# Windowed attention and a SiLU feed-forward layer on one core: new loads for batch 0, and pieces of batches 1 and 2 moved among blocks of 256

## The chip, the cores and the metric

The kernel runs on one core of a Trainium2 chip. The core has five engines that run their own queues of instructions in order and wait for each other by semaphores: TensorE (PE, matrix products and transposes), VectorE (DVE), ScalarE (ACT), GpSimd (POOL, which here mostly issues loads) and SyncE (SP, which issues stores). Transfers run on 16 DMA engines. The metric is the device time of one execution in microseconds; less is better. Before the change the median of 3 runs is 331.06 us (330.93 to 331.69).

## What is computed

Attention over 8 batches, 8 heads, 576 tokens and 64 elements a head. In heads 0 to 3 a token sees itself and the 31 tokens before it ("plain"). In heads 4 to 7 it sees every fourth token of the last 128 ("strided"): tokens of one residue modulo 4 form a class of 144, and within a class the window is again 32. The result, 4608 rows of 512, goes through a feed-forward layer with SiLU.

```python
rel = pos[:, None] - pos[None, :]
mask_plain = (rel >= 0) & (rel < 32)
mask_dil = (rel >= 0) & (rel < 128) & (rel % 4 == 0)
scores = np.where(mask, scale * q @ k.T, -1e9)
attn = np.exp(scores - scores.max(-1))
attn = attn / (attn.sum(-1) + 1e-9)
x = (attn @ v)                        # 4608 x 512
h = x @ w_in                          # 512 -> 2048
out = (h / (1 + np.exp(-h))) @ w_out  # 2048 -> 512
```

## The kernel before

**Attention.** q and k of a batch are loaded by GpSimd's queue (with a cast to float16) into `n` tiles, several tokens a partition (`load_qk`, L102; batch 0 in two parts of 256 and 320 tokens with 8 tokens a partition, `load_qk0`, L114). TensorE transposes them into PSUM (`transpose`, L260; batch 0: `transpose0`, L288 and L296). Copies bring them to `kT`, `qT` (plain) or `kC`, `qC` (strided). For later batches the copies are `both`: half 0 by VectorE, half 1 by ScalarE. A score block is 32 queries by 64 keys, four blocks above each other on the partitions (`score` L306, `score_class` L318). VectorE scales and adds the mask (L369, L379 for batch 0; L415, L424) and takes the negated maximum of each block (L389, L431). Then `exps` has two forms. Without `shift`, ScalarE runs one exp for each block of 64 columns with the maximum as bias and the sum as a second output (L459, each with an instruction that reads the sum). With `shift` (L441), VectorE subtracts the maxima first, ScalarE runs one exp over all blocks (L453), and VectorE sums afterwards (L468). `normal` divides (L472, L473, L475), `turn` transposes the weights (L484), `turned` copies them (L492), `values` multiplies by V (L517; batch 0: L543; the last 64 tokens: L580), `finish` copies the result to `xT` (L593; batch 0: L556).

**V.** `vw` holds V in windows of 64 rows. `load_v` (L123, L131, L136) fills the upper half of the partitions; `shift_v` (L146, L151, L154, L156) copies rows from there to the lower half by SBUF-to-SBUF DMAs, on SP's queue for batches 0 and 1. `clear_v` zeroes the rows that no load fills.

**Feed-forward.** `layer1` multiplies by `w_in` (L606, SiLU on ScalarE L614; batch 0 in two parts, L625 and L632), with two PSUM tiles `h`. `layer2` multiplies by `w_out` (L666, for batch 0 L642), `store` copies out and SP stores (L651, L652). Even batches have 4 row tiles in the second layer, odd ones 5.

**Order.** It is written out by hand. Batch 0's attention up to the first values stands ahead of the loop. After that, attention of later batches is put between the matmuls of the feed-forward layers: `plan_of(b)` fills a list of steps, and `plan(s)` issues what is due. Steps 0 to 15 are the 16 blocks of the first layer of batch b, steps from 16 on are groups of 4 matmuls of its second layer. What is added first at a step is issued first. In steps 15 to 18 of batch 1:

```python
transposes(at, 3, 0, 15)
at(17, load_qk, 4)
at(14, scores, 2, 1)
all_exps(2, 0)      # at step 16
all_exps(2, 1)      # at step 16
at(17, scores, 3, 0)
at(18, exps, 3, 0, 0)
at(18, exps, 3, 0, 1)
```

PSUM holds two `big` tiles (h, o and batch 0's scores) and four `ps` tiles (transposes, scores, values). `keep_busy` issues matmuls whose result nobody reads. A load on GpSimd's queue waits until the eighth load before it has landed.

Of the kernel before, what the change touches and what calls it, by code (L numbers as in the profile page):

```python
# [22 lines left out]
UR = 8  # L23
# [4 lines left out]
def kernel(  # L28
# [62 lines left out]
    def load_qk(b):  # L91

        for which in (0, 1):
            t = nat.tile([P, H * UR, D], F16, tag=f"n{which}", name=f"n{which}_{b}")
# [12 lines left out]
    def load_qk0(part):  # L107

        t0, n = ((0, PA), (SA, PB))[part]
        qk0[part] = [None, None]  # L110
        for which, src in ((1, k), (0, q)):
            t = nat.tile([P, H * UR, D], F16, tag=f"n{which}", name=f"n{which}_0{part}")
            t = qk0[part][which] = t.rearrange("p (h u) d -> p h u d", h=H)
            nc.gpsimd.dma_start(  # L114
                out=t[0:n],
                in_=src[0, :, t0 : t0 + n * UR].rearrange("h (p u) d -> p h (u d)", u=UR),
            )
# [23 lines left out]
    def shift_v(b, queue, parts):  # L141
# [3 lines left out]
        for m0, m1, n in parts:  # L145
            queue.dma_start(  # L146
                out=vw[W:KB, NP + n.start * ND : NP + n.stop * ND],
                in_=vw[KB : KB + W, NP + n.start * ND : NP + n.stop * ND],
            )
            if n.stop == 2:  # L150
# [3 lines left out]
            queue.dma_start(out=f[W:KB, :, m0:m1], in_=f[KB : KB + W, :, m0:m1])  # L154
            l0 = max(m0, 1)
            queue.dma_start(out=f[0:W, :, l0:m1], in_=f[KB + W : P, :, l0 - 1 : m1 - 1])  # L156

    FIRST, REST, ALL = (0, 4, slice(0, 1)), (4, NM, slice(1, 2)), (0, NM, slice(0, 2))
# [36 lines left out]
    load_qk0(0)  # L195
    make_identity(nc, ident)

# [8 lines left out]
    load_qk0(1)  # L206
    load_v(0, ("first", "plain"))
    load_w_in(0)
    load_v(0, ("second", "short"))
    shift_v(0, nc.sync, (FIRST, REST))  # L210
    clear_v(1, nc.gpsimd)
    for c in range(1, 4):
        load_w_in(c)
# [222 lines left out]
    def shift(b, z, hi):  # L436
# [4 lines left out]
        nc.vector.tensor_tensor(  # L441
# [248 lines left out]
    def plan_of(b):  # L690
# [9 lines left out]
        if b == 0:  # L700
# [16 lines left out]
            at(10, scores, 1, 1)  # L717
            for hi in (0, 1):
                at(10, shift, 1, 1, hi)
            transposes(at, 1, 0, 13)  # L720
            at(17, scores, 1, 0)
# [5 lines left out]
            for hi in (0, 1):  # L727
                at(17, exps, 1, 0, hi)
            later(at, 1, 1, (18, 20, 24, 26))
            later(at, 1, 0, (22, 25, 28, 30))  # L730
        elif b == 1:
            at(16, load_v, 3)
            at(16, shift_v, 3, nc.gpsimd, (ALL,))
            transposes(at, 2, 0, 4)
            transposes(at, 2, 1, 10)
            transposes(at, 3, 0, 15)
            at(7, scores, 2, 0)
            at(17, load_qk, 4)
            at(14, scores, 2, 1)
            all_exps(2, 0)  # L740
            all_exps(2, 1)
            at(17, scores, 3, 0)
            at(18, exps, 3, 0, 0)
            at(18, exps, 3, 0, 1)
            later(at, 2, 0, (22, 24, 27, 28))
            later(at, 2, 1, (29, 31, 33, 34))
        else:
# [36 lines left out]
    def keep_busy(n):  # L784

        busy = big.tile([P, 2, 512], F32, tag="big", name="busy")
        four = ident[:, None, :].broadcast_to([P, 4, P])
        for _ in range(n):
            nc.tensor.matmul(busy[:, 0].rearrange("p (n c) -> p n c", n=4), ident, four, start=True, stop=True)

    load_qk(1)
    load_w_out(0)
# [4 lines left out]

    transposes0(0, 1, (act, dve))
    scores0(1, 0)
    transposes0(0, 0, (act, dve))  # L800
    exps(0, 1, 0)
    scores0(0, 0)
    transposes0(1, 1, (act, dve))
    exps(0, 0, 0)
    normal(0, 1, 0)
    scores0(1, 1)
    turn(0, 1, 0)
    turned(0, 1, 0, act)
    transposes0(1, 0, (act, act))
    normal(0, 0, 0)  # L810
    turn(0, 0, 0)
    turned(0, 0, 0, act)
    shift(0, 1, 1)
# [60 lines left out]
```

## Time and profile before

| what | us |
|---|---|
| median of 3 runs (range) | 331.06 (330.93 to 331.69) |
| the profiled execution | 331.63 |
| its span, first to last instruction | 329.8 |
| TensorE busy | 311.1 (94%) |
| ScalarE busy | 214.8 (65%) |
| VectorE busy | 180.2 (55%) |
| GpSimd busy | 86.0 (26%) |
| first matmul of the first layer (L625) starts | 25.69 |
| second layer of batch 0 (L642) starts | 47.68 |
| first layer of batch 1 (L606) starts | 67.36 |
| second layer of batch 1 (L666) starts | 89.06 |

In the rows of the profile a line names engine, source line, operation and tiles ("t<-ident,n": t is written from ident and n), then the count. In the row of slices, 40 equal pieces of 8.2 us, a digit is the busy share in tenths. In a table of stretches each row has from and to, the length, and busy time with the number of instructions for TensorE, its weight loads, VectorE, ScalarE and GpSimd, then the granted TensorE clock, the share of the DMA engines and GB/s. In a timeline, a row has start, length, and in brackets the idle time of the engine before it with what ended it. The source lines named in this section are those of the kernel before.

### The profile page before, as it was taken

The page shows a single profiled execution, that of the slowest core. Times are in us where ns is not written, and L with a number is a line of the kernel's source. Part 1 is how long each engine was busy: PE and PEld are TensorE (multiplying, and loading weights), DVE is VectorE, ACT ScalarE, POOL GpSimd, SP SyncE. Part 2 cuts the span into 40 slices and gives each one's busy share as a digit, 9 for nine tenths or more (in the row PEclk, how much of TensorE's full clock was granted, in tenths as well). Part 3 has the DMA queues.
Part 4 walks back from the last instruction along what each step waited for, and adds up shares of the span by engine and source line. Part 5 has one row for each costly group of instructions (what it writes and reads, how often), then busy time and mean ns, then how long its engine had stood idle before and what let it go on. Part 6 is the DMA issues. An engine that isn't in the chain of part 4 may idle for free.

```text
span 329.8 us, 11976 instructions
## 1 busy us (share of the span) xinstructions
PE 311.1 (94%) x5238; PEld 203.1 (62%) x5238; DVE 180.2 (55%) x377; ACT 214.8 (65%) x714; POOL 86.0 (26%) x144
## 2 busy tenths in 40 slices
PE   1679999999899999999999999999999999999996
PEld 1547764577545777467845677468755676467644
DVE  5778379745578744774557444774557442540011
ACT  2746669156599847985699357995699447916400
POOL 8743645544500560056004430042000000000000
PEclk9999999999999999999999999999999999999999
DMA  6999999999911975199404990175001100110022
GB/s 92 168 216 198 166 204 210 191 204 107 166 47 70 137 108 98 67 107 175 70 34 92 177 143 6 64 101 108 2 34 66 66 4 1 64 66 2 0 76 86
DMA packets 45141, 32.90 MB, mean 100 GB/s; under 512 B 21824, under 2 KB 39744, under 8 KB 45088
## 3 DMA queue, kind: packets, MB, share of 16 engines
q0 software_dynamic: 38752, 21.74, 48.5%
q1 hardware_dynamic: 6336, 10.39, 8.8%
q8 instruction: 41, 0.67, 0.9%
q14 instruction: 12, 0.10, 0.1%
HBM read 37.75 MB, written 9.44 MB: 143 GB/s over the span
## 4 chain that ended last, share of the span: by engine, by line
PE 79%; DMA 10%; DVE 4%; ACT 3%; POOL 2%; issue 2%; POOLq 0%
PE h L606 34%; PE o L666 31%; DMA n<-in_k_dram 4%; DMA vw<-in_v_dram 3%; PE t L260 3%; DMA n<-in_q_dram 3%; PE x L517 3%; PE pt L484 2%; ACT pe L459 2%; PE o L642 2%; PE s L318 1%; PE s L306 1%; DVE ms L415 1%; DVE pn L475 1%; DVE nm L431 1%
## 5 line engine op out<-in xcount | busy, mean ns | idle before, releaser
L614 ACT ACTIVATE gT<-h 128x576 f16<-128x576 f32 x112 | 72.8, 650 | 72.1 <-PE h L606 71.4
L606 PE MATMUL h<-xT,w_in 128*128 128x288 f16 x896 | 115.5, 286 | 0.8 <-issue 0.4
L666 PE MATMUL o<-w_out,gT 128*128 128x512 f16 (+1 forms) x528 | 115.6, 373 | 0.0
L606 PEld LDWEIGHTS <-w_in 128*128 128x128 f16 x896 | 85.7, 98 | 24.0 <-issue 1.3
L459 ACT ACTIVATE pe<-ms,nm 128x64 f32<-128x64 f32 x262 | 86.9, 334 | 0.1
L666 PEld LDWEIGHTS <-gT 128*128 128x128 f16 x528 | 50.0, 98 | 53.0
L651 DVE COPY ob<-o 128x512 f32<-128x512 f32 (+1 forms) x37 | 24.9, 674 | 53.6 <-PE o L666 53.1
L459 ACT ACTIVATION_READ_ACCUMULATOR pe<-ms,nm 128x1 f32 x262 | 49.2, 188 | 0.0
L415 DVE SCALAR_TENSOR_TENSOR ms<-s,mask 128x512 f32<-128x512 f32 x28 | 19.2, 686 | 39.1 <-PE ss L306 19.0
L123 POOL DMA_DIRECT2D vw<-in_v_dram x16 | 10.0, 632 | 84.8 <-PE x L517 84.3
L475 DVE TENSOR_TENSOR pn<-pe,r 128x640 f16<-128x640 f32 (+2 forms) x32 | 25.3, 792 | 1.1
L593 DVE CAST xT<-x 128x512 f16<-128x512 f32 x28 | 18.0, 686 | 11.7 <-PE xs L580 11.7
L431 DVE TENSOR_REDUCE nm<-ms 128x10 f32<-128x640 f32 (+1 forms) x28 | 22.0, 787 | 1.0
L102 POOL DMA_DIRECT2D n<-in_q_dram x28 | 16.4, 605 | 13.5 <-DMA w_in<-in_moe_w_in_dram 5.7
L102 POOL DMA_DIRECT2D n<-in_k_dram x28 | 16.5, 604 | 8.1 <-DMA w_in<-in_moe_w_in_dram 2.8
L492 DVE COPY ptT<-pt 128x640 f16<-128x640 f16 (+2 forms) x30 | 13.1, 472 | 9.9 <-PE pt L484 9.7
L625 PE MATMUL h<-xT,w_in 128*128 128x256 f16 (+1 forms) x128 | 17.8, 293 | 0.0
L632 ACT ACTIVATE gT<-h 128x512 f16<-128x512 f32 (+1 forms) x16 | 10.4, 650 | 8.1 <-PE h L625 7.9
L642 PE MATMUL o<-w_out,gT 128*128 128x512 f16 x64 | 14.8, 379 | 0.0
L625 PEld LDWEIGHTS <-w_in 128*128 128x128 f16 x128 | 12.3, 100 | 3.8 <-issue 0.5
L260 PEld LDWEIGHTS <-n 64*64 64x64 f16 (+1 forms) x840 | 10.0, 101 | 6.4 <-issue 5.1
L484 PE MATMUL pt<-ident,pn 128*128 128x128 f16 x152 | 12.2, 224 | 1.7 <-DVE pn L475 1.7
(84 smaller groups left out, 261.6 us busy)
## 6 DMA issues: line engine op xcount, KB each, us to landing
out_dram<-ob SPq DMA_DIRECT2D x35, 256.0 KB, 2.0
n<-in_k_dram POOLq DMA_DIRECT2D x28, 144.0 KB, 5.4
n<-in_q_dram POOLq DMA_DIRECT2D x28, 144.0 KB, 5.7
vw<-in_v_dram POOLq DMA_DIRECT2D x8, 288.0 KB, 7.0
vw<-in_v_dram POOLq DMA_DIRECT2D x16, 128.0 KB, 4.4
w_in<-in_moe_w_in_dram POOLq DMA_DIRECT2D x4, 512.0 KB, 12.5
w_out<-in_moe_w_out_dram POOLq DMA_DIRECT2D x4, 512.0 KB, 11.3
vw<-vw POOLq DMA_DIRECT2D x12, 128.0 KB, 3.7
```

The lines of the kernel that those rows point to most:

```text
L102: nc.gpsimd.dma_start(out=qk[b, z, which][i * HF : i * HF + UPS[z]].rearrange("p h u d -> p h (u d)"), in_=src[b, h : h + 2].rearrange("h ...
L260: nc.tensor.transpose(dst, w, ident[r, r])
L415: nc.vector.scalar_tensor_tensor(out=ms[:, 0:8].rearrange("p (n t) c -> p n (t c)", n=2), in0=s[hi].rearrange("p n t c -> p n (t c)"), sca ...
L431: nc.vector.tensor_reduce(out=nm[:, 0:w], in_=ms[:, 0:w], axis=AX.X, op=ALU.max, negate=True)
L459: nc.scalar.activation(pe[:, t, :], ms[:, t, :], AF.Exp, bias=nm[:, t : t + 1], accum_out=l[:, t : t + 1],)
L475: nc.vector.tensor_tensor(pn[:, 0:w], a["pe", z, hi][:, 0:w], r[:, 0:w, None].broadcast_to([P, w, KB]), ALU.mult)
L606: nc.tensor.matmul(h[:, half, 0:HS], w_in16[:, c, f * P : f * P + P], xT[:, c, half * HS : half * HS + HS], start=(c == 0), stop=(c == MC ...
L614: nc.scalar.activation(gT[:, f, s0 : s0 + S].rearrange("p (a c) -> p a c", a=2), h[:, :, 0:HS], AF.Silu)
L625: nc.tensor.matmul(h[:, i, 0 : c1 - c0], w_in16[:, c, (f + i) * P : (f + i + 1) * P], xT[:, c, c0:c1], start=(c == 0), stop=(c == MC - 1),)
L642: nc.tensor.matmul(o, gT[:, f, t * P : (t + 1) * P], w_out16[:, f, :], start=(f == 0), stop=(f == NFF - 1),)
L651: nc.vector.tensor_copy(ob, o)
L666: nc.tensor.matmul(o[:, 0, 0:m], gT[:, f, t * P : (t + 1) * P], w_out16[:, f, cols], start=(f == 0), stop=(f == NFF - 1),)
```

## The change

Batch 0's q and k come with 4 tokens a partition instead of 8: 64 and 80 partitions instead of 32 and 40, in pieces of 1 KB instead of 2 KB; in the first part the strided heads are loaded ahead of the plain ones, in DMAs of their own. The first four plain windows of batch 0's V are shifted by two VectorE copies instead of two DMAs. GpSimd subtracts the maxima of (0, plain, part 0), which had none subtracted before, and of (0, strided, part 1). The order of batch 0's attention is new, the first values are plain ones, both exps of part 1 stand after the first `finish`, and `keep_busy` is gone. On GpSimd's queue w_in 1 stands behind its first subtraction, w_in 2 and 3 behind its second; `load_qk(1)` and `clear_v(1)` follow these. In the plan of batch 0, batch 1's plain transposes go from step 13 to 17 and their scores from 17 to 20, with VectorE subtracting the second maximum; in the plan of batch 1, batch 3's plain transposes go from step 15 to 17, their scores from 17 to 20, their exps from 18 to 21. Some other steps move by one.

```diff
-UR = 8
+UR = 4
...
-    def load_qk0(part):
+    def load_qk0(part, kinds):
...
+        for h in kinds:
+            for which, src in ((1, k), (0, q)):
+                nc.gpsimd.dma_start(
+                    out=qk0[part][which][0:n, h].rearrange("p h u d -> p h (u d)"),
+                    in_=src[0, h, t0 : t0 + n * UR].rearrange("h (p u) d -> p h (u d)", u=UR),
+                )
...
+            move = getattr(queue, "dma_start", None) if queue in (nc.sync, nc.gpsimd) else queue.tensor_copy
+            move(out=f[W:KB, :, m0:m1], in_=f[KB : KB + W, :, m0:m1])
             l0 = max(m0, 1)
-            queue.dma_start(out=f[0:W, :, l0:m1], in_=f[KB + W : P, :, l0 - 1 : m1 - 1])
-
-    FIRST, REST, ALL = (0, 4, slice(0, 1)), (4, NM, slice(1, 2)), (0, NM, slice(0, 2))
+            move(out=f[0:W, :, l0:m1], in_=f[KB + W : P, :, l0 - 1 : m1 - 1])
+
+    FIRST, REST, ALL = (0, 4, None), (4, NM, slice(1, 2)), (0, NM, slice(0, 2))
+    STRIDED_FIRST = (0, 0, slice(0, 1))
...
-    load_qk0(0)
+    load_qk0(0, (STRIDED,))
     make_identity(nc, ident)
+    load_qk0(0, (PLAIN,))
...
-    load_qk0(1)
+    load_qk0(1, (slice(0, H),))
     load_v(0, ("first", "plain"))
+    shift_v(0, nc.sync, (STRIDED_FIRST,))
     load_w_in(0)
     load_v(0, ("second", "short"))
-    shift_v(0, nc.sync, (FIRST, REST))
-    clear_v(1, nc.gpsimd)
-    for c in range(1, 4):
-        load_w_in(c)
+    shift_v(0, nc.sync, (REST,))
...
-    def shift(b, z, hi):
+    def shift(b, z, hi, engine=nc.vector):
...
-            at(10, scores, 1, 1)
+            at(8, scores, 1, 1)
             for hi in (0, 1):
-                at(10, shift, 1, 1, hi)
-            transposes(at, 1, 0, 13)
-            at(17, scores, 1, 0)
+                at(8, shift, 1, 1, hi)
+            transposes(at, 1, 0, 17)
+            at(20, scores, 1, 0)
+            at(20, shift, 1, 0, 1)
...
             for hi in (0, 1):
-                at(17, exps, 1, 0, hi)
+                at(20, exps, 1, 0, hi)
             later(at, 1, 1, (18, 20, 24, 26))
-            later(at, 1, 0, (22, 25, 28, 30))
+            later(at, 1, 0, (25, 26, 28, 30))
...
-            transposes(at, 2, 0, 4)
+            transposes(at, 2, 0, 3)
             transposes(at, 2, 1, 10)
-            transposes(at, 3, 0, 15)
-            at(7, scores, 2, 0)
+            transposes(at, 3, 0, 17)
+            at(8, scores, 2, 0)
             at(17, load_qk, 4)
-            at(14, scores, 2, 1)
+            at(13, scores, 2, 1)
             all_exps(2, 0)
             all_exps(2, 1)
-            at(17, scores, 3, 0)
-            at(18, exps, 3, 0, 0)
-            at(18, exps, 3, 0, 1)
+            at(20, scores, 3, 0)
+            at(21, exps, 3, 0, 0)
+            at(21, exps, 3, 0, 1)
...
-                at(9, scores, b + 1, 1)
+                at(10, scores, b + 1, 1)
...
-                transposes(at, b + 2, 1, 30)
+                transposes(at, b + 2, 1, 31)
...
+    transposes0(0, 1, (act, dve))
+    scores0(1, 0)
+    transposes0(0, 0, (act, dve))
+    exps(0, 1, 0)
+    scores0(0, 0)
+    shift(0, 0, 0, nc.gpsimd)
+    load_w_in(1)
+    transposes0(1, 1, (act, act))
+    exps(0, 0, 0)
+    transposes0(1, 0, (act, act))
+    normal(0, 1, 0)
+    normal(0, 0, 0)
+    scores0(1, 1)
+    shift(0, 1, 1, nc.gpsimd)
+    for c in (2, 3):
+        load_w_in(c)
+    turn(0, 1, 0)
+    turned(0, 1, 0, act)
+    shift_v(0, nc.vector, (FIRST,))
+    scores0(0, 1)
+    turn(0, 0, 0)
+    turned(0, 0, 0, act)
+    shift(0, 0, 1)
+    values0(0, 0)
+    finish0(0, 0, (act, act))
+    values0(1, 0)
+    finish0(1, 0, (act, act))
+    exps(0, 1, 1)
+    exps(0, 0, 1)
     load_qk(1)
+    clear_v(1, nc.gpsimd)
     load_w_out(0)
     load_w_out(1)
     load_v(1)
     load_w_out(2)
     load_w_out(3)
...
     load_qk(2)
```

More of the change, by code (lines that the diff above doesn't have):

```diff
@@ L93, in load_qk @@
         for which in (0, 1):
-            t = nat.tile([P, H * UR, D], F16, tag=f"n{which}", name=f"n{which}_{b}")
+            t = nat.tile([P, 2 * sum(URS), D], F16, tag=f"n{which}", name=f"n{which}_{b}")
             u0, u1 = 2 * URS[0], 2 * (URS[0] + URS[1])
@@ L105, in load_qk @@
                     )
-    def load_qk0(part):
+    def load_qk0(part, kinds):
         t0, n = ((0, PA), (SA, PB))[part]
[L110 to L117, printed above, removed]
+        if part not in qk0:
+            tiles = [nat.tile([P, 2 * sum(URS), D], F16, tag=f"n{w}", name=f"n{w}_0{part}") for w in (0, 1)]
+            qk0[part] = [t[:, 0 : H * UR].rearrange("p (h u) d -> p h u d", h=H) for t in tiles]
+        for h in kinds:
[4 more added lines that the diff above has]
+                )
     def load_v(b, pieces=("first", "second", "short", "plain")):
@@ L145, in shift_v @@
         for m0, m1, n in parts:
[L146 to L150, printed above, removed]
+            if n:
+                queue.dma_start(
+                    out=vw[W:KB, NP + n.start * ND : NP + n.stop * ND],
+                    in_=vw[KB : KB + W, NP + n.start * ND : NP + n.stop * ND],
+                )
+            if n and n.stop == 2:
                 queue.dma_start(
@@ L153, in shift_v @@
                 )
-            queue.dma_start(out=f[W:KB, :, m0:m1], in_=f[KB : KB + W, :, m0:m1])
+            if m1 == m0:
+                continue
+            move = getattr(queue, "dma_start", None) if queue in (nc.sync, nc.gpsimd) else queue.tensor_copy
+            move(out=f[W:KB, :, m0:m1], in_=f[KB : KB + W, :, m0:m1])
             l0 = max(m0, 1)
-            queue.dma_start(out=f[0:W, :, l0:m1], in_=f[KB + W : P, :, l0 - 1 : m1 - 1])
-    FIRST, REST, ALL = (0, 4, slice(0, 1)), (4, NM, slice(1, 2)), (0, NM, slice(0, 2))
+            move(out=f[0:W, :, l0:m1], in_=f[KB + W : P, :, l0 - 1 : m1 - 1])
+    FIRST, REST, ALL = (0, 4, None), (4, NM, slice(1, 2)), (0, NM, slice(0, 2))
+    STRIDED_FIRST = (0, 0, slice(0, 1))
     def plain_v(a, j, h):
@@ L194 @@
     clear_v(0, nc.vector)
-    load_qk0(0)
+    PLAIN, STRIDED = slice(0, HH), slice(HH, H)
+    load_qk0(0, (STRIDED,))
     make_identity(nc, ident)
+    load_qk0(0, (PLAIN,))
     nc.gpsimd.affine_select(
@@ L440, in shift @@
         ms, nm = a["ms", z, hi], a["nm", z, hi]
-        nc.vector.tensor_tensor(
+        engine.tensor_tensor(
             ms[:, 0:w], ms[:, 0:w], nm[:, 0:w, None].broadcast_to([P, w, KB]), ALU.add
@@ L782, in transposes0 @@
                 transpose0(part, 2 * z + i, which, copies[which])
[L784 to L789, printed above, removed]
+    transposes0(0, 1, (act, dve))
[27 more added lines that the diff above has]
+    exps(0, 0, 1)
     load_qk(1)
+    clear_v(1, nc.gpsimd)
     load_w_out(0)
@@ L796 @@
     load_w_out(3)
[L798 to L813, printed above, removed]
-    exps(0, 1, 1)
-    scores0(0, 1)
-    shift(0, 0, 1)
-    keep_busy(4)
-    values0(1, 0)
-    finish0(1, 0, (dve, act))
-    values0(0, 0)
-    finish0(0, 0, (dve, act))
-    exps(0, 0, 1)
-    keep_busy(2)
     load_qk(2)
```

## The prediction, made before the changed kernel ran

> **What bounds the kernel now.** First the busy times and the slices of the page, then the stretches, to see where TensorE stands still.
>
> ```profile
> PE 311.1 (94%) x5238; PEld 203.1 (62%) x5238; DVE 180.2 (55%) x377; ACT 214.8 (65%) x714; POOL 86.0 (26%) x144
> ...
> PE   1679999999899999999999999999999999999996
> ...
> DMA  6999999999911975199404990175001100110022
> ```
>
> ```profile
> 0.00:10.00 10.00, 3.29 (x120) 2.95 (x122) 5.65 (x24) 1.93 (x3) 8.75 (x20) 1.00 0.78 105
> 10.00:20.00 10.00, 6.87 (x239) 5.38 (x236) 7.78 (x17) 8.83 (x42) 5.87 (x8) 1.00 1.46 184
> 20.00:25.69 5.69, 3.96 (x86) 1.65 (x76) 3.75 (x7) 2.11 (x5) 2.29 (x4) 1.00 1.22 219
> ...
> 66.70:89.00 22.30, 20.59 (x474) 15.67 (x473) 11.60 (x20) 13.06 (x21) 12.30 (x21) 1.00 1.04 156
> 89.00:110.00 21.00, 21.00 (x327) 10.80 (x326) 14.76 (x34) 20.69 (x115) 1.89 (x4) 1.00 0.27 73
> ```
>
> TensorE is the bound from 25.69 us, where the first layer starts, and its idle time (18.7 us of 329.8) lies mostly before that. What can be won is that start, and 1.7 us between 66.7 and 89. The last line is the one to keep: from 89 to 110, the second layer of batch 1, TensorE has no idle time at all and ScalarE works 20.69 of 21.00 us. The timeline there, TensorE and then ScalarE:
>
> ```profile
> 85.47 0.48 PE L260 MATMUL t<-ident,n 64*64 64x64 f16 x36
> 86.86 0.67 PE L260 MATMUL t<-ident,n 64*64 64x64 f16 x36 [0.91 <-DVE ms L415]
> 87.46 0.91 PE L606 MATMUL h<-xT,w_in 128*128 128x288 f16 x6
> 88.82 0.41 PE L606 MATMUL h<-xT,w_in 128*128 128x288 f16 x2 [0.45 <-issue]
> 89.06 1.02 PE L666 MATMUL o<-w_out,gT 128*128 128x512 f16 x4
> 90.02 0.68 PE L306 MATMUL s<-kT,qT 64*32 64x64 f16 x64
> ```
>
> ```profile
> 89.26 0.65 ACT L614 ACTIVATE gT<-h 128x576 f16<-128x576 f32 x1 [0.96 <-PE h L606]
> 89.93 1.28 ACT L459 ACT_TABLE_LOAD   x1
> 91.22 0.35 ACT L459 ACTIVATE pe<-ms,nm 128x64 f32<-128x64 f32 x1
> ```
>
> ```profile
> L459 ACT ACTIVATE pe<-ms,nm 128x64 f32<-128x64 f32 x56 | 18.6, 337 | 0.0
> ```
>
> Batch 3's plain transposes (step 15) wait 0.91 us for buffers that VectorE still reads. Their copies on ScalarE are done before the table load at 89.93; then 56 exps run without a gap, the last starting at 109.46: (109.46 − 91.22) / 55 = 0.332 us each.
>
> **The decisive part: batch 3's transposes go from step 15 to 17.** `exps` of batch 2 stay at step 16: 8 + 10 + 10 + 10 = 38 exps with a bias for each block. `transposes` uses `both`: half 0 is copied by VectorE, half 1 by ScalarE. At step 17 the two ScalarE copies (kT, qT) stand behind the 38 exps on an engine that works in order; the built order of the changed kernel shows table load, x8, x10, x10, x10, kT, qT. TensorE meets `scores(3, 0)` at step 20, and those read half 1. Let L be the start of this second layer (89.06 before). TensorE gets there after 4 matmuls (0.86), 72 transposes (0.76 at 71.44 in the chain) and 12 matmuls (2.60): L + 4.2. ScalarE starts its exps at 91.22 − 89.06 = L + 2.16, needs 38 × 0.332 = 12.6, then two copies (72.02 to 73.20, 1.2): L + 16.0. TensorE stands **11.8 us**. Bounds 11.0 (half 0's scores go first, copies overlap) and 12.5 (the exps' own 337 ns, 12.8, and full copies). Behind the blocked scores stand all later second-layer matmuls; before, none had slack, so nothing takes this back.
>
> After such a pause the matmuls may run at half pace. The start of the trace shows it, though the granted clock reads 1.00:
>
> ```profile
> 22.07 1.89 PE L789 MATMUL busy<-ident 128*128 128x512 f16 x4
> ```
>
> Four matmuls of 512 columns take 1.89 us there and 1.02 at 89.06. The slow pace lasted until about 26.5 (4 first-layer matmuls from 25.69 to 26.50, 5 in the next 0.5), 4.4 us in all, of which 3.5 dense. Bounds 0 and 2.2 (half of 4.4); I take 1.7, half of the dense part, the nearest row. The Trainium skill (TensorE: Matmul & The Clock Gate, Part 1) says that an idle window of about 3.4 us halves the clock until a window as long has been busy. By that rule the pause here costs 1.7, without it 0; the slow start agrees, and no pause of this length in mid-kernel is in this trace.
>
> **The start.** Loads: the first part is 64 rows of 4 tokens instead of 32 of 8, strided heads first, so transposes halve (16 for 0.61 before, 8 now; plain 64 for 1.89, 32 now). GpSimd issues two more DMAs (2 × 0.66 by its rows) ahead of the band, which stays in front of the first mask-add. k,q of part 1 keep their bytes at twice the descriptors; on each of the 16 engines v's first 16 pieces of 1 KB took 1.0 (it landed at 14.4, q01 at 13.4), 62 ns a piece, and w_in's 32 pieces of 2 KB 3.4 (landings near 23.7, 27.0, 30.6), 106 ns: 2304 pieces at 62 instead of 1152 at 106 are +1.3. Against that, 80 rows divide evenly among 16 engines and 40 do not (k01 was used 4.1 after q00, q01 only 2.3 after k01). I put q01 at 12.8 instead of 13.4; bounds 11.5 and 14.7.
>
> Chain from there, durations of equal instructions before: part-1 copies on ScalarE to 14.0 (two of 0.4 after the transposes); exp(0,0) 0.65 to 14.7; VectorE sum, add, reciprocal, product 0.69 + 0.17 + 0.20 + 0.69, with gaps to 16.5; (1,1) mask-add and maximum 0.6 + 0.45 + 0.95 to 18.5; the two V copies that replace DMAs; (0,1) mask-add 0.6 + 0.3, which frees the buffer that the second values need; values 0.65, two copies on ScalarE 0.8. V copies of 1024 and 768 elements: by the 512-element copy L222 (0.43) 0.86 + 0.65; the lower bound is two of the 64-element copies L221 (0.213 each), 0.4, the upper 0.96 + 0.72 (memset L190, 0.485 for 512). The SP queue loses the two plain shifts (issued at 16.86 and 17.56), and the strided one, alone now, lands its median 5.3 after v's 13.8, before the values. The six filler matmuls (2.9 us) lay in the wait for those shifts: 0. I take 1.5 for the copies: first layer at 22.5, **−3.2** (bounds −5.0 and +0.5).
>
> GpSimd's subtractions of 512 and 768 columns: lower bound VectorE's own 0.69 and 0.95, upper twice its select's rate (0.287 for 128), 2.3 and 3.4; I take that rate once, 1.2 and 1.7. The Trainium skill (GPSIMD Engine Reference, Performance versus the Vector engine) gives 2.6 cycles an element for two inputs, by which 1.1 and 1.7 would be my estimate; no run here shows it. The first is hidden under the eight exps of (1,0) (2.7 us) and the wait for q01; the second under the V copies and (0,1). But w_in 2 and 3 are queued behind the second: issue at about 20.4 and 21.2 instead of 13.70 and 14.76. Cover: the DMA queue is full until w_in 1 lands (23.7, the wait that ends at 23.72 on GpSimd), so they still land near 27 and 30.6; needed at about 28.6 and 31.5. The clear of vw1 (3.3) now stands before w_out 0; batch 1's q,k keep the queue full meanwhile: 0.
>
> **First layer, batch 0.** ScalarE now runs exps (1,1) and (0,1), 0.85 + 0.74, and the table load 1.28 before its first silu: 2.9 after the layer's start, against 27.38 − 25.69 = 1.7. With two h buffers TensorE follows: **+1.2**. Batch 1's plain transposes leave step 13, where they waited 0.80 at 45.02: **−0.8**; their own 0.95 is paid at step 17: 0. Batch 3's load waits on GpSimd for them, but its turn came at 54.38 anyway: 0.
>
> **Second layer, batch 0.** `scores(1, 0)` at step 20 wait for ScalarE (silu, table 1.28, two exps 1.4, copies 1.2): about 0.35. VectorE then has mask-adds, maxima and the new subtraction (3.9 us) ahead of `normal(1,1,1)` (2.05), so `turn` at 24 waits about 2.0 (0.77 before); `normal(1,0,1)`, now at 26 behind the copies of `values`, makes `turn` at 28 wait about 1.7. New 4.05 less old 0.44 + 0.77 + 0.39: **+2.4** (bounds 0 and 4).
>
> **First layer, batch 1.** Without transposes at 15 the waits 0.91 and 0.45 go: **−1.36**. Scores and transposes moved by one step (batch 2 on, and 9 to 10, 30 to 31 later) stand beside a TensorE without waits: 0, bounds ±0.5.
>
> **Sum.** −3.2 + 1.2 − 0.8 + 2.4 − 1.36 + 11.8 + 1.7 = +11.7. The profiled execution took 331.63 (span 329.8 and 1.83 around it), so 343.4; the median of the runs shown is 0.57 lower: **342.8**.
>
> **Rivals.** (1) Faster: ScalarE's copies don't hold TensorE. This needs the 38 exps done by L + 4.2, or 0.05 us each; then pause and slow matmuls go, 331.06 − 1.8 = **329.3**. For it: `scores` of half 0 need VectorE's copies alone. Against: half 1 follows in the same in-order queue, and 56 exps without a gap. (2) Slower still: the weights behind GpSimd's subtraction come late. With a median landing of 12.5 us from issue, w_in 2 lands at 32.9, 4.3 after its need: **347.1**. For it: the queue's own issue order; against: that landing time is queueing, most of it. It decides once the queue runs empty before 21. (3) A better start: V copies at 0.4, subtractions at VectorE's pace, first layer at 20.7, and half of the new `turn` waits: 342.8 − 1.8 − 1.2 = **339.8**.
>
> **Chances.** Forecast 0.68, (1) 0.06, (2) 0.13, (3) 0.13. The range holds the forecast with its bounds, (3), and (2) in part: **337.5 to 347**. Low end: the start's −1.8, the second layer's −2.4 and no slow matmuls (−1.7) together are −5.9, not all at once; high end +3.7, +1.6, +0.5 likewise. Only (1) is faster, 0.07 with what I have not seen; within 0.3% (1 us, about what a measurement tells) 0.02; slower 0.91.
>
> **What would show it.** In the second layer of batch 1 the profile should have a gap of 11 to 12 us on TensorE, inside scores that wait for ScalarE's copy of qT, with 38 exps of 0.33 before it; 16 or so slow matmuls after it; the first h near 22.5; waits at `turn` in batch 0's second layer; w_in 2 and 3 issued after 20. I am wrong if TensorE runs through that layer, if copies are not held by exps, or if the first layer waits for w_in.

## The result, and the profile after

The changed kernel takes **346.84 us** (median of 4 runs, 346.34 to 347.32), beside 331.33 (330.93 to 331.69) for the kernel before on the same chip: a ratio of 1.0468, with a 95% interval of 1.0447 to 1.0490. Predicted were 342.8 and a range of 337.5 to 347. Medians and ranges are over all runs of a kernel; the ratios leave out runs in a slower state, with a lower granted clock, so a ratio need not be the quotient of two medians shown. The profiled execution took 347.32, with a span of 345.5, 15.7 longer than before.

The page of the changed kernel, with the slices of TensorE's busy share and granted clock:

```profile
PE 312.7 (90%) x5136; PEld 202.0 (58%) x5136; DVE 183.1 (53%) x377; ACT 211.5 (61%) x684; POOL 90.1 (26%) x148
...
PE   3669997799808999999999999999999999999996
...
PEclk9999998999956999999999999999999999999999
```

TensorE is busy 1.6 us longer (312.7 against 311.1), with 102 matmuls fewer; the other 14.1 of the 15.7 are idle time. The slices have a hole at the 12th, where the digit is 0, and the granted clock is low there and behind it, and once ahead of it. Two stretches of the changed kernel, the second layer of batch 0 and that of batch 1, and then a table of all stretches:

```profile
44.04:68.72 24.68, 20.58 (x382) 10.25 (x380) 19.36 (x39) 9.08 (x24) 13.03 (x23) 0.93 1.31 203
88.69:124.23 35.54, 24.29 (x398) 11.93 (x396) 16.61 (x36) 23.22 (x117) 1.76 (x3) 0.81 0.18 45
```

| stretch | before | after | difference |
|---|---|---|---|
| start, up to the first layer | 25.69 | 22.18 | -3.51 |
| first layer of batch 0 | 21.99 | 21.86 | -0.13 |
| second layer of batch 0 | 19.68 | 24.68 | +5.00 |
| first layer of batch 1 | 21.70 | 19.97 | -1.73 |
| second layer of batch 1 | 20.80 | 35.54 | +14.74 |
| the rest | 219.94 | 221.27 | +1.33 |

(The cuts are not quite alike. Two matmuls of the first layer run at 21.41 already, and the table takes the next, at 22.18; by the very first matmul the start gains 4.28. And the 47.68 of before is a weight load; the first matmul of that second layer starts at 47.81. By first matmuls, the first two layers of batch 0 change by +0.50 and +5.13.)

In the start, the first values wait 1.15 and 1.25 us for the two copies of V that VectorE now makes. VectorE and GpSimd there:

```profile
17.91 0.42 DVE L159 COPY vw<-vw 32x1024 f16<-32x1024 f16 x1
17.98 1.69 POOL L447 TENSOR_TENSOR ms<-ms,nm 128x768 f32<-128x768 f32 x1 [4.48 <-DVE nm L395]
18.36 1.51 DVE L161 COPY vw<-vw 32x768 f16<-32x768 f16 x1
```

The copy of 1024 elements takes 0.42 us, the one of 768 takes 1.51 and ends 0.2 us behind GpSimd's subtraction. It does so in all ten traces that have this copy on VectorE (1.51 each, 0.20 to 0.22 behind the subtraction). A small addition on VectorE that takes 0.17 us elsewhere takes 0.84 to 0.85 beside GpSimd's first subtraction, in ten traces too, and ends 0.03 behind it. So these instructions of VectorE end only when GpSimd's is done, and the change has put them into the same moment. At the pace of the first copy the second would take about 0.32 (an estimate), so this costs the start about 1.2. Not all of VectorE's work is held up: in the kernel with four more edits, below, a mask-add beside the subtraction takes its usual 0.68. That GpSimd is what the copy waits for is read from the ten traces; no run has the two apart on VectorE.

The large loss lies where the prediction put it. TensorE's timeline in the second layer of batch 1, and the chain that ended last over the same time:

```profile
90.40 2.76 PE L672 MATMUL o<-w_out,gT 128*128 128x512 f16 x12
93.10 0.31 PE L312 MATMUL s<-kT,qT 64*32 64x64 f16 x32
104.65 0.41 PE L312 MATMUL s<-kT,qT 64*32 64x64 f16 x32 [11.25 <-ACT qT L270]
...
105.17 8.71 PE L672 MATMUL o<-w_out,gT 128*128 128x512 f16 x28
```

```profile
98.39 5.16 ACT pe L465 x31
103.55 0.52 ACT kT L270
104.07 0.54 ACT qT L270
...
104.65 0.41 PE s L312 x32
```

The scores of half 0 run at 93.10. Those of half 1 wait 11.25 us for ScalarE's copy of qT, which stands behind the exps in its queue. The 28 matmuls that follow take 8.71, 0.311 each; the 12 ahead of the pause take 2.76, 0.230 each. Of the 14.74, 11.25 are the wait, 2.65 this slow pace (8.71 less 6.06 at the pace of 0.216 that matmuls of this shape have elsewhere) and 0.83 batch 3's transposes, which moved in from the stretch before.

Three more stretches of the changed kernel show the granted clock by itself (the first number behind the last bracket):

```profile
55.65:59.06 3.41, 3.41 (x13) 1.16 (x10) 1.59 (x5) 0.00 (x0) 3.12 (x6) 0.50 1.15 201
93.20:96.61 3.41, 0.21 (x32) 0.09 (x27) 0.69 (x1) 3.41 (x22) 0.00 (x0) 1.00 0.20 77
96.61:110.26 13.65, 5.61 (x52) 2.23 (x53) 3.96 (x8) 8.88 (x49) 0.00 (x0) 0.50 0.01 1
```

The clock is either full or half, in pieces of 3.41 us, and half follows a piece in which TensorE did little: here 0.21 us of work. It stays at half until 110.26, 5.6 us behind the pause. It is at half from 55.65 too, and that was not foreseen; the piece ahead of that has 1.05 us of work. The wait ahead of it, in the second layer of batch 0:

```profile
55.43 0.55 PE L490 MATMUL pt<-ident,pn 128*128 128x128 f16 x5 [2.36 <-DVE pn L481]
55.78 3.51 PE L648 MATMUL o<-w_out,gT 128*128 128x512 f16 x8
```

Eight matmuls take 3.51 behind it, and 1.89 further on. The same place before:

```profile
56.75 0.45 PE L484 MATMUL pt<-ident,pn 128*128 128x128 f16 x5 [0.77 <-DVE pn L475]
57.04 1.89 PE L642 MATMUL o<-w_out,gT 128*128 128x512 f16 x8
```

### The profile page after: what moved, and what is told of

It reads as the page before. It is cut to its first block, busy times and chain, and to the rows that moved or that the text cites. A ratio compares the mean times of both kernels' runs of the same rounds, so it can differ in the third digit from the quotient of the medians.

```text
span 345.5 us, 11738 instructions
## 1 busy us (share of the span) xinstructions
PE 312.7 (90%) x5136; PEld 202.0 (58%) x5136; DVE 183.1 (53%) x377; ACT 211.5 (61%) x684; POOL 90.1 (26%) x148
## 4 chain that ended last, share of the span: by engine, by line
PE 79%; ACT 7%; DVE 7%; DMA 3%; issue 2%; POOL 1%; POOLq 0%; DVEq 0%
PE h L612 32%; PE o L672 29%; ACT pe L465 6%; PE h L631 4%; PE t L266 3%; PE x L523 2%; PE o L648 2%; PE pt L490 2%; DMA n<-in_q_dram 2%; DVE pn L481 1%; PE s L324 1%; PE s L312 1%; DMA out_dram<-ob 1%; DVE l L474 1%; POOL n L115 1%
## 5 line engine op out<-in xcount | busy, mean ns | idle before, releaser
L672 PE MATMUL o<-w_out,gT 128*128 128x512 f16 (+1 forms) x528 | 118.3, 379 | 0.0
L465 ACT ACTIVATE pe<-ms,nm 128x64 f32<-128x64 f32 x244 | 81.0, 333 | 8.2 <-DVE pn L481 5.9
L465 ACT ACTIVATION_READ_ACCUMULATOR pe<-ms,nm 128x1 f32 x244 | 45.5, 187 | 0.0
L631 PE MATMUL h<-xT,w_in 128*128 128x256 f16 (+1 forms) x128 | 19.1, 302 | 0.9 <-issue 0.5
L102 POOL DMA_DIRECT2D n<-in_q_dram x28 | 16.4, 600 | 12.7 <-DMA w_out<-in_moe_w_out_dram 6.2
L312 PE MATMUL s<-kT,qT 64*32 64x64 f16 x512 | 6.1, 202 | 12.6 <-ACT qT L270 11.2
L648 PE MATMUL o<-w_out,gT 128*128 128x512 f16 x64 | 16.6, 410 | 0.0
```

Source lines behind the costliest of these rows:

```text
L102: nc.gpsimd.dma_start(out=qk[b, z, which][i * HF : i * HF + UPS[z]].rearrange("p h u d -> p h (u d)"), in_=src[b, h : h + 2].rearrange("h ...
L465: nc.scalar.activation(pe[:, t, :], ms[:, t, :], AF.Exp, bias=nm[:, t : t + 1], accum_out=l[:, t : t + 1],)
L631: nc.tensor.matmul(h[:, i, 0 : c1 - c0], w_in16[:, c, (f + i) * P : (f + i + 1) * P], xT[:, c, c0:c1], start=(c == 0), stop=(c == MC - 1),)
L648: nc.tensor.matmul(o, gT[:, f, t * P : (t + 1) * P], w_out16[:, f, :], start=(f == 0), stop=(f == NFF - 1),)
L672: nc.tensor.matmul(o[:, 0, 0:m], gT[:, f, t * P : (t + 1) * P], w_out16[:, f, cols], start=(f == 0), stop=(f == NFF - 1),)
```

## The experiments

The kernel before runs between 329.6 and 338.8 us on the chips of the experiments. So each kernel is compared by its ratio to runs of the kernel before on its own chip, and places are compared within the traces.

### Batch 3's pieces back

```diff
-            transposes(at, 3, 0, 17)
+            transposes(at, 3, 0, 15)
-            at(20, scores, 3, 0)
-            at(21, exps, 3, 0, 0)
-            at(21, exps, 3, 0, 1)
+            at(17, scores, 3, 0)
+            at(18, exps, 3, 0, 0)
+            at(18, exps, 3, 0, 1)
```

> The changed kernel with batch 3's pieces back in their old steps (transposes 15, scores 17, exps 18); all else stays changed. Theory: the wait of 11.25 us ahead of the scores of (3, plain) and the 2.65 us of matmuls at half pace behind it both come from this one move, so the time falls by 13.9, from 346.84 to about 333 (1 us to either side), and what is left against before, 1.6 us, is the second layer of batch 0 less the gain of the start. The old waits of 0.91 and 0.45 in the first layer of batch 1 may come back, which would make it up to 334.3. Rival: the loss comes from the whole rearrangement (other pieces of batches 1 and 2, loads), and the wait only moves to the next piece: over 342.

Measured: 336.56 (332.94 to 340.84), ratio 1.005 (1.000 to 1.010) against 1.0468 for the whole change. The scores of (3, plain) run with no wait, and the 40 matmuls behind them take 8.81, 0.220 each. By the ratios, undoing this one move takes away 0.042 of the 0.047, nine tenths of the loss.

### Batch 3's pieces alone, in the kernel before

The same lines, the other way round, in the kernel before.

> The kernel before with nothing changed but batch 3's pieces (transposes to step 17, scores to 20, exps to 21). Theory: this alone makes the large loss: 331.3 + 11.3 for the wait + 2.65 for the matmuls at half pace - 1.36 for the two waits that leave the first layer of batch 1 = 343.9 (342.5 to 345). Rival: the wait needs another moved piece as well, such as the exps of batch 2 coming later; then it stays under 335.

Measured: 344.87 (342.60 to 346.53), ratio 1.0295 (1.0236 to 1.0355).

```profile
105.00 0.41 PE L306 MATMUL s<-kT,qT 64*32 64x64 f16 x32 [9.41 <-ACT qT L264]
```

The wait for ScalarE's copy is 9.41; 1.70 us of another wait, of which more below, stands among the transposes ahead of it, and the 28 matmuls behind it take 8.97. The move is enough by itself to make the wait. By the ratio it brings 0.030 of the 0.047, less than its undoing takes away; the kernel before spreads from 329.64 to 336.45 on this chip, and the runs do not settle the share more closely.

### Batch 3's pieces moved, their copies on VectorE

```diff
-            transposes(at, 3, 0, 17)
+            for which in (1, 0):
+                at(17, transpose, 3, 0, which, (dve, dve))
```

> The changed kernel with batch 3's transposes still at step 17 and its scores at step 20, but with both halves copied by VectorE instead of half 1 by ScalarE. Theory: it is not the step that costs, but that ScalarE's two copies stand behind 38 exps (38 x 0.332 = 12.6 us) in its in-order queue. VectorE's queue is short there, so the wait of 11.25 shrinks to under 1 us and the matmuls keep their pace: about 333.3 (332.5 to 335). Rival: the transposes come too late for the scores whoever copies them, because VectorE itself waits or because the PSUM tiles are held: over 340.

Measured: 333.44 (332.07 to 335.59), ratio 1.0046 (1.0001 to 1.0090). TensorE at the same place:

```profile
94.29 0.68 PE L312 MATMUL s<-kT,qT 64*32 64x64 f16 x64
...
94.98 6.22 PE L672 MATMUL o<-w_out,gT 128*128 128x512 f16 x28
```

Steps and order are those of the change, and 64 scores of both halves run in one go. What cost 14 us is therefore not that the transposes come at step 17, but that two copies of 0.5 us stand behind 38 exps in ScalarE's queue.

### The pause filled with matmuls

```diff
+            at(20, fill, 45)
             at(20, scores, 3, 0)
```

> The changed kernel with 45 more matmuls of 512 columns whose result nobody reads (45 x 0.216 = 9.7 us) in the pause of 11.25 us ahead of the scores of (3, plain). Theory: the 2.65 us that the 28 matmuls behind the pause take beyond full pace come from the idle TensorE, whose granted clock there reads 0.63; kept busy, it runs them in 6.06 instead of 8.71, so the time falls by 2.2 to 2.65, to about 344.3, though nothing waits less. Rival: the slow pace has nothing to do with idleness (operands, ports or the transfers at that place): 346.8, with the same 8.7 us for the 28 matmuls, or more by what the added matmuls delay.

```profile
93.30 9.88 PE L701 MATMUL busy<-ident 128*128 128x512 f16 x45
...
104.95 0.32 PE L312 MATMUL s<-kT,qT 64*32 64x64 f16 x32 [1.53 <-ACT qT L270]
...
105.38 6.22 PE L672 MATMUL o<-w_out,gT 128*128 128x512 f16 x28
```

The 28 matmuls behind the pause take 6.22 instead of 8.71, and the clock is full there, so the slow pace is one of idleness. The Trainium skill (TensorE: Matmul & The Clock Gate, Part 1) speaks of a free-running window of 3413 ns, and the pieces of 3.41 agree. The whole time does not settle what this is worth: the median of 348.03 (345.28 to 351.41) is not lower than 346.84, the ratio of 1.0367 (1.0292 to 1.0442) is lower than 1.0468. In the profiled run, new waits of 2.06 at 140.68 and 1.36 at 179.66 stand in this kernel, which no semaphore explains.

### Batch 1's pieces back

```diff
-            at(8, scores, 1, 1)
+            at(10, scores, 1, 1)
-            transposes(at, 1, 0, 17)
-            at(20, scores, 1, 0)
-            at(20, shift, 1, 0, 1)
+            transposes(at, 1, 0, 13)
+            at(17, scores, 1, 0)
...
-            later(at, 1, 0, (25, 26, 28, 30))
+            later(at, 1, 0, (22, 25, 28, 30))
```

> The changed kernel with batch 1's pieces in the plan of batch 0 back in their old steps (strided scores 10, plain transposes 13, plain scores and exps 17, normals from 22) and without VectorE's subtraction of the second maximum. Theory: the second layer of batch 0 loses its new waits ahead of the turns (2.36 and 1.37) and the half pace behind the first (1.6), some 5 in all, and gets its old waits back (0.44 + 0.77 + 0.39), while the wait of 0.80 for the transposes comes back in the first layer: 346.84 - 5.3 + 1.6 + 0.8 = about 343.9 (342.5 to 344.5). Rival: these waits hide others that show as soon as they go (the store tile, the copies for the first layer of batch 1): under 1 us gained, over 345.8.

Measured: 348.19 (346.43 to 349.31), ratio 1.0482 (1.0427 to 1.0536). Nothing is gained, where 2.9 us were expected. The second layer of batch 0 is 5.63 shorter, as expected (19.05 against 24.68). But the first layer, from its first matmul at 21.81 to 50.02, takes 28.21 against 22.63 (21.41 to 44.04) in the changed kernel. Only 0.80 and 0.95 of this are the wait and the transposes that were expected there. The rest begins in this line:

```profile
46.51 3.67 PE L631 MATMUL h<-xT,w_in 128*128 128x320 f16 x14 [2.45 <-issue]
```

TensorE waits 2.45 us for nothing that the profile shows, and works at half the clock from 46.42 to 49.83, which makes these 14 matmuls 1.6 slower.

### The new start alone

All pieces in their old steps; the loads, GpSimd's subtractions and the order of batch 0's attention as changed.

> The new start (loads with 4 tokens a partition, GpSimd's two subtractions, shifts by VectorE, new order of batch 0's attention) with every piece of the plans in its old step. Theory: the start gains 3.5 us and gives 1.2 back in the first layer of batch 0, where ScalarE runs two exps and a table load ahead of the first SiLU; nothing else differs from before: 331.3 - 2.3 = 329.0 (328.3 to 330.0). Rival: the earlier start only meets the weights or batch 1's q and k earlier, all of it comes back as a wait by the end of batch 0's first layer: 331 or more.

```profile
46.99 3.89 PE L631 MATMUL h<-xT,w_in 128*128 128x320 f16 x14 [2.18 <-issue]
```

Measured: 339.08 (337.88 to 340.49), ratio 1.0217 (1.0173 to 1.0261), far off what was expected. The start, by its first matmul, is 3.1 earlier (22.56 against 25.69), and the stretch up to the second layer takes 28.1 where before takes 22.0. The clock is at half from 46.10 to 52.93 and from 93.88 to 97.29. Both follow waits of the same nameless kind, the 2.18 shown and one of 1.38 at 93.24.

### The start alone, batch 3's transposes one step later

```diff
-            transposes(at, 3, 0, 15)
+            transposes(at, 3, 0, 16)
             all_exps(2, 0)
```

> The start alone with one more step moved: batch 3's plain transposes at step 16, ahead of the exps of batch 2, instead of 15. Theory: ScalarE's two copies then still stand ahead of the 38 exps in its queue, so no long wait appears, and the two waits of 0.91 and 0.45 that the transposes at 15 caused in the first layer of batch 1 go: 1.36 less than the start alone, at most. Rival: the copies delay the first exps by their 1.1 us or the waits come back at step 16, where the same transposes wait for the same buffers: the same as the start alone, within 0.3. A long wait (over 5 us) would say that the exps are not what the copies stood behind.

Measured: 337.52 (335.43 to 338.38), ratio 1.0177 (1.0134 to 1.0219), 1.56 under the start alone, with intervals that overlap. No wait for ScalarE's copies appears: the transposes stand in the same step as the exps, but ahead of them, and that is early enough. Of the waits at these transposes, 0.91 and 1.38 in the start alone, one of 1.02 without a name stays.

### The start alone, with 8 tokens a partition

```diff
-UR = 4
+UR = 8
```

(The tiles of q and k are widened to hold it.)

> The start alone with 8 tokens a partition again (pieces of 2 KB on half as many partitions, all else new). Theory: four tokens a partition double the partitions that a load reaches, and with these the DMA engines at work, so q of part 0 lands earlier; with 8 the scores of part 0 and with them the first layer start about 1 us later: 1.1 more than the start alone (0.5 to 1.6). Rival: larger pieces move faster, or the first layer waits for V and the normals and not for q and k: no difference (within 0.4) or a gain.

Measured: 335.77 (332.74 to 336.20), ratio 1.0100 (1.0054 to 1.0147): not slower than the start alone but 1% faster. The start itself is 1.77 later (24.33 against 22.56), a little more than expected. q of part 0 is not late, as the theory had it; q of part 1 is used 1.13 later (14.58 against 13.45), and VectorE's copies of V end 1.13 later with it. The other 0.6 comes with this wait:

```profile
22.05 0.27 PE L490 MATMUL pt<-ident,pn 128*128 128x128 f16 x1 [2.68 <-issue]
```

The wait without a name stands here, and the one at 47 us is gone.

### What these waits are: instructions

A view of the changed kernel's page counts what TensorE's instruction queue moves:

```profile
q8 instruction: 40, 0.66, 0.8%
```

Forty packets of some 16.4 KB, for 10272 matmuls and weight loads: one packet for 257. Below are ten of the nameless waits, with the last packet before each and its position, the number of TensorE's records of all kinds that start ahead of it in the trace:

```
kernel          packet            TensorE goes on   wait   position
before           19.47 -  20.45    21.93            1.73     705
before           86.38 -  87.27    88.82            0.45    3265
after            30.65 -  31.61    33.14            0.46     961
after           210.35 - 211.30   212.67            0.69    6849
batch 3 alone    90.21 -  91.17    92.43            1.70    3265
batch 1 back     44.12 -  45.09    46.51            2.45    1473
start alone      44.58 -  45.54    46.99            2.18    1473
start alone      90.79 -  91.77    93.24            1.38    3009
8 tokens         19.51 -  20.52    22.05            2.68     705
pause filled    138.41 - 139.38   140.68            2.06    4545
```

Every position is 193 plus a multiple of 256, and TensorE goes on 1.26 to 1.55 us after the end of the packet. The same holds for every wait of 0.25 us or more that the profile calls "issue" at a matmul of TensorE in the 14 traces: 34 waits, all at such positions, 1.26 to 1.71 behind a packet. So these are waits at the end of a page of 256 instructions for the next page. A packet takes 0.9 to 1.1 us, but ahead of these waits it starts 2.2 to 4.6 us behind the end of the page before (in the start alone: page end at 40.80, packet at 44.58). By these numbers a page then has to last about 6.2 us (3.8 + 1.0 + 1.4), and 128 matmuls of 64 columns with their weight loads go by in about 1.5 (at 72 in 0.83). The Trainium skill (Runtime: NRT & Kernel Launch, Instruction fetch mechanics) has the blocks of 256 instructions and calls the cost of crossing one mostly hidden; here it is up to 2.68 us, and the measurement decides.

With the old steps, the new start brings batch 1's 72 transposes and 80 scores into the 4 us in which the packet is on its way, and the page ends before the next is there. The change's own steps (transposes at 17, scores at 20) spread them, and the changed kernel has no wait there. This is what batch 1's move was worth here, and why undoing it gained nothing.

### The ends of the pages moved, in the start alone

```diff
     transposes0(0, 1, (act, dve))
+    pad(74)
```

> The start alone with 74 small matmuls (64 by 64, result not read) added behind the first transposes, where TensorE waits 1.4 us for copies anyway. New theory: the waits of TensorE that no semaphore explains (2.48 us at 46.99 in the start alone, 1.57 at 93.24) are waits for its own instructions. They all lie at instruction 193 + a multiple of 256 of TensorE's trace and end 1.3 to 1.5 us after a 16 KB packet of the instruction queue; the packet is asked for one page (256 instructions) earlier and comes 3 to 4 us later while loads fill the DMA engines. 148 more instructions move the ends of the pages into stretches of long matmuls, so these waits go, and with the first the 3.4 to 6.8 us at half pace behind it. Expected: 6 us under the start alone, 0.998 to 1.006 of the kernel before instead of 1.022. Rival: the waits are for data or buffers that the trace fails to name (the copies of the moved transposes, w_in's last part); then 74 more matmuls change nothing at 47, and the ratio stays at 1.02 or gets worse.

```profile
51.42 0.30 PE L312 MATMUL s<-kT,qT 64*32 64x64 f16 x28 [2.00 <-issue]
```

Measured: 336.37 (334.58 to 338.25), ratio 1.0100 (0.9989 to 1.0211), under the start alone, though the intervals overlap. The wait of 2.18 at the 14 first-layer matmuls is gone, which the rival excluded: that page now ends at the first of batch 1's transposes, with a wait of 0.44. But the next one ends inside the scores at 51.42, at position 1729, its packet starting 4.46 after the page end before. So the waits stayed at page ends and moved to other work, and the gain of 6 us was too much to expect from that. The added matmuls also took 4.15 us, and the first layer starts 1.1 later.

### The ends of the pages moved, in the kernel before

```diff
     transposes0(0, 1, (act, dve))
+    pad(116)
```

> The kernel before with 116 small matmuls (64 by 64, result not read) behind its first transposes, nothing else changed. New theory: its wait of 1.73 ahead of the scores of part 0 at 21.93 is one for instructions as well (they arrive 1.48 ahead of its end); with the ends of the pages moved by 232 instructions it is under 0.6. But V's shifts by DMA land behind it, so the first layer starts at most 0.5 earlier, at 25.2 to 25.7, and the time stays within 1 us of before: 0.997 to 1.002. Rival: the page set the start of the first layer, which then comes at 24.0 or earlier, and the time falls by 1.7 or more; a good part of what the changed start gains would then be that its loads with 4 tokens a partition need fewer transposes, 102 TensorE matmuls less.

Measured: 336.52 (336.16 to 337.75), ratio 1.0115 (0.9999 to 1.0231). This one does not answer its question: the added matmuls took 6.39 us where TensorE had little idle time, the first layer started at 30.54 instead of 25.69, and a page wait (1.18 at 22.69) was there all the same, at the same position 705, with other work behind it.

### One normal ahead of VectorE's scores work

In the kernel with batch 3's copies on VectorE:

```diff
-            later(at, 1, 1, (18, 20, 24, 26))
+            later(at, 1, 1, (18, 19, 24, 26))
```

> The changed kernel with batch 3's copies on VectorE (as in an earlier run: 333.4) and one more edit: the second normal of (1, strided) at step 19 instead of 20, so that it stands ahead of VectorE's mask-adds, maxima and subtraction for (1, plain) and not behind them. Theory: the wait of 2.25 at the turn of step 24 comes from those 3.85 us of VectorE work alone; it goes, while the copies of the turned weights and the turn of step 28 now wait about 1.2 and 1.4 for the same VectorE. The second layer of batch 0 takes 22.2 instead of 24.4 (21.5 to 23.0), and the time falls by 2 us. Rival: VectorE's queue is full in that stretch whatever the order, and the waits at later turns take up all that the first one gives: 24 or more, no gain.

```profile
55.16 0.72 PE L490 MATMUL pt<-ident,pn 128*128 128x128 f16 x10
...
63.05 0.45 PE L490 MATMUL pt<-ident,pn 128*128 128x128 f16 x5 [1.61 <-DVE pn L481]
```

Measured: 331.77 (330.79 to 333.51), ratio 0.9991 (0.9948 to 1.0033), against 1.0046 (1.0001 to 1.0090) without the edit; the intervals overlap, and the trace has to tell. The ten transposes of the turn run in one go, with no wait; the later turn waits 1.61. The second layer of batch 0 takes 21.57 instead of 24.42, and its clock is full. VectorE does the same work in both: in these two traces its order alone made 2.85 us, the half pace included that the longer wait had brought.

### Four more edits together

On top of the last kernel:

```diff
-    o32 = ctx.enter_context(tc.tile_pool(name="o32", bufs=3))
+    o32 = ctx.enter_context(tc.tile_pool(name="o32", bufs=4))
...
-    shift_v(0, nc.vector, (FIRST,))
+    shift_v(0, nc.scalar, (FIRST,))
...
-    load_w_in(1)
+    for c in (1, 2, 3):
+        load_w_in(c)
...
-            later(at, 1, 0, (25, 26, 28, 30))
+            ev[26].remove((finish, (1, 1)))
+            at(26, finish, 1, 1, act)
+            at(25, normal, 1, 0, 0)
+            at(26, normal, 1, 0, 1)
+            later(at, 1, 0, (-99, -99, 28, 30))
```

> The kernel of the normal at step 19 with four more edits, each against a wait that its trace shows: the two shifted copies of V by ScalarE, which is idle from 19.9 to 23.1 there, instead of VectorE, behind whose mask-adds they stand (waits of 1.76 and 1.25 at the first values); w_in 2 and 3 issued ahead of GpSimd's second subtraction; the copies of the finish of (1, strided) by ScalarE, so that VectorE reaches the last normal of (1, plain) sooner (wait of 1.61 at the turn of step 28); a fourth tile for the stores (waits of 0.36 and 1.22 on the store's transfer). Theory: TensorE follows each of these waits one for one, so the first layer starts 1.7 earlier, the second layer of batch 0 is 1.4 shorter and the first layer of batch 1 1.2 shorter: 4.3 in all, 0.984 to 0.991 of the kernel before. Rival: the earlier start only meets w_in, SiLU or the instruction pages sooner, and of the 4.3 under 1.5 is left: 0.995 or more.

```profile
19.44 1.07 PE L549 MATMUL x<-ptT,vw 64*64 64x32 f16 x64 [1.97 <-ACT ptT L498]
```

Measured: **326.94** (325.98 to 327.50) beside 334.74 (330.62 to 338.76), ratio **0.9827** (0.9783 to 0.9872), faster than both kernels. The first values wait once, 1.97, instead of 1.76 and 1.25, and the first layer starts at 20.79 against 24.03. Of these 3.24, 1.78 are there ahead of any of the edits: q of part 1 is used at 13.15 in this trace and at 14.93 in the other. The second layer of batch 0 takes 20.00 (21.57), the first layer of batch 1 19.00 (20.38), with TensorE busy for all of the 19.00. These four edits were tried only together; the traces say which stretches became shorter, not how much each edit is worth alone.

## Why the prediction was right, point by point

- **Start: predicted -3.2, measured -3.5 (-4.3 by the very first matmul).** In part this is luck. q of part 1 is used at 12.31 (12.8 predicted), the earliest of the eight traces with the same loads and the same order in the start: they go from 12.31 to 14.93, and the first matmul from 21.41 to 24.03, 22.3 in the middle. GpSimd's subtractions take 1.04 and 1.69 (1.2 and 1.7; the estimate by the Trainium skill, GPSIMD Engine Reference, Performance versus the Vector engine, was 1.1 and 1.7). The second comes so near only beside VectorE's copies; without them, in the last experiment, it takes 1.47. VectorE's two copies take 0.42 and 1.51 (0.86 and 0.65). Their sum is 0.4 above the predicted one, and for a reason that was left out: the prediction put the second subtraction at nothing because it would be hidden under these copies, and one of them ended only behind it, about 1.2 late. With that, rival (3) falls: it wanted both copies at 0.4 and subtractions at VectorE's pace. w_in 2 and 3 are issued at 19.61 and land by 27.32 and 30.82; TensorE waits for neither, so rival (2) falls.
- **First layer of batch 0: +1.2 and -0.8, and 0.95 of transposes moved out; measured -0.13.** That leaves +1.6 for what was put at 1.2. Of it, 0.9 stands where the prediction said, at the 17th matmul, which waits for the first SiLU (3.28 us behind the start of the layer, before 2.36), and 0.46 is a page wait at 33.14. The number is about right, the reason incomplete: batch 1's new steps were credited with a wait of 0.8 saved here, and the kernel with the old ones shows that they saved 5.6, because TensorE would have run out of instructions. As that never happened in the kernel before, the sum does not show the error.
- **Second layer of batch 0: predicted +2.4 and the 0.95, measured +5.0.** The waits at the turns were right: 2.36 and 1.37 (2.0 and 1.7). The 0.35 for the scores did not come. Of the old waits, 0.44 was a weight load's, beside which matmuls ran on, and 0.39 a page wait (position 2241). What was left out follows the first turn: eight matmuls at half the clock, 1.6, which the prediction counted only behind the long pause.
- **First layer of batch 1: -1.36, measured -1.73 with 0.83 of transposes moved out.** The waits of 0.91 and 0.45 went, but the 0.45 was a page wait (position 3265), not one for the transposes' buffers. New is a wait of 0.81 for a store's tile, not foreseen.
- **The stall: predicted 11.8, measured 11.25.** The queue, the 38 exps and the copies are as described; the copies on VectorE and the move alone show it. Rival (1), that copies do not hold TensorE, falls.
- **Slow matmuls behind it: predicted 1.7, bounds 0 and 2.2, measured 2.65.** Out of its bounds: the clock stayed at half for 5.6 us behind the pause, not 4.4, and matmuls ran densely for all of it. The mechanism was right and the size was not: the piece in which the pause ends (103.44 to 106.85) was not busy enough to end the half pace, so the next one ran at half as well.
- **Rest: predicted 0 within 0.5, measured +1.33.** The scores at the page wait of 0.69 at 212.67 lose 0.87 in all. In the first layers of batches 3 and 5 the third block starts 0.18 later each: the transposes that moved from step 30 to 31 put ScalarE's two copies right ahead of its table load, and the first SiLU starts 1.46 behind the start of batch 3's layer, before 1.18. A move by one step, put at 0, cost 0.4.

With the moved transposes (0.83 to 0.95 for each set) set against each stretch, the terms missed by -0.3 in the start, +0.4 in the first layer of batch 0, +1.7 in its second, +0.5 and +0.4 in the two layers of batch 1 and +1.3 in the rest. These 4.0 are the way from 343.4, the sum against the profiled execution, to 347.3. They nearly all add up on one side, which is why the time lies at the upper end of the range, 0.16 below its top; and the early q helped: in the three other kernels that share all of batch 0's first layer (batch 3's pieces back, its copies on VectorE, the pause filled), the first matmul comes 0.8 to 1.3 later and the second layer of batch 0 starts 0.15 to 0.67 later. So the mechanism of the large loss was right, and that the whole lies within the range owes something to luck.

## What to carry to other kernels

Before a step is moved later, look at what the queue of each engine that it uses holds from there on: copies of 0.5 us behind 38 exps cost 14 us, and the same copies on another engine cost nothing. A wait of TensorE that the profile calls "issue" should be checked against its position in the instruction stream: when it falls on a page end, TensorE has run through small matmuls faster than its pages come under loads, and spreading them was the remedy here. Two engines that work at the same moment are to be looked at as well, not only one after the other: a copy estimated at 0.32 took 1.51 beside GpSimd's subtraction. And a move that loses time in one stretch may be what keeps another stretch running, so undo each part alone before it is called a loss.

## What the runs showed of the hardware

- TensorE waited for its own instructions, up to 2.68 us at a time, at page ends of 256 instructions, with the packet starting up to 4.6 us behind the page end before. Which page end falls on a dense stretch changes with every instruction added or removed ahead of it. That a quicker packet would end these waits was not tried.
- A wait of 2.36 us, shorter than one clock piece of 3.41, was enough to halve the next piece. The low pieces of the changed kernel start 40.96 apart, 12 times 3.41, and in the five other kernels with two low stretches the starts are whole multiples of 3.41 apart too. So the pieces lie on a grid, and where a wait falls in it decides what it costs. In the 14 traces, each of the 16 full-clock pieces that are followed by a half one has at most 1.44 us of TensorE work, and no full piece with 1.53 or more is followed by a half one. Two near the limit, the first (kernel of the 74 added matmuls) followed by half, the second (batch 3's pieces alone) by full:

```profile
49.45:52.86 3.41, 1.44 (x41) 0.83 (x41) 0.89 (x2) 2.12 (x3) 0.60 (x2) 1.00 1.21 245
94.06:97.47 3.41, 1.53 (x38) 0.58 (x36) 0.69 (x1) 3.41 (x22) 0.00 (x0) 1.00 0.16 59
```

- The added matmuls of 64 by 64 took 55 ns each (6.39 for 116), transposes of that size 11.5 (72 in 0.83). The first all have the same operands and write the same place, and they run in the slow pace of the start; which of these makes the difference was not tried.
- On VectorE a float16 copy (1.51 us, where some 0.3 is the estimate) and a small addition (0.84, elsewhere 0.17) ended only when GpSimd's subtraction beside them was done, in ten traces each.
